# Nine softmax groups a pair, weight chunks converted partly by Prelu passes, and a new order of steps

## Chip, cores and metric

The kernel runs on one core of one Trainium2 chip. The metric is the device time of one execution in microseconds (us); a run's number is the median of several executions, and the number of this kernel is the median of three runs.

## What is computed

Two stages follow each other. Attention of 8 batches with 8 heads, 576 queries of 64 numbers each, where keys and values are first averaged over 8 neighbours, so that each query has 72 keys. Its output, 4608 rows of 512 numbers, then goes through a root-mean-square norm and a gated layer with 1536 hidden columns:

```python
k_p = k.reshape(B, H, 72, 8, D).mean(axis=3)           # B = H = 8, D = 64
v_p = v.reshape(B, H, 72, 8, D).mean(axis=3)
scores = scale * q @ k_p.T                             # 576 x 72 for each head
scores = scores - max(scores, axis=-1)
attn = exp(scores); attn = attn / (sum(attn, axis=-1) + 1e-9)
x = concat_heads(attn @ v_p)                           # 4608 x 512
xn = x / sqrt(mean(x * x, axis=-1) + 1e-6) * rms_g
g = xn @ w_gate                                        # 512 x 1536
val = xn @ w_val
out = (g * sigmoid(g) * val) @ w_out                   # 1536 x 512
```

The three weight matrices come as 64-bit floats, the rest as 32-bit floats.

## The kernel before

**Precision.** A product of 32-bit floats is made of three matmuls: each factor is split into a rounded high part ("hi", a copy into the type fp32r) and the remainder ("lo", a subtraction), and hi x hi, lo x hi and hi x lo are added in PSUM. The copy is mostly on ScalarE (ACT), the subtraction on GpSimd (POOL) or VectorE (DVE).

**Weights.** They arrive in 26 chunks, 16 of 512 and 10 of 1024 columns on 128 partitions (`CHUNKS`), as pairs of 32-bit words. A chunk takes six steps: `w_load` (a DMA, tile `wx`), `w_abs` (ACT, L316, the high word scaled by a power of two, into tile `wt`), `w_shift` (DVE, L320, three bits to the left), `w_low` (DVE, L324, the low word's bits joined in), `w_sign` (DVE, L328, the sign bit joined in), `w_hi` (ACT, L342, the rounded copy into `w`), and `w_lo` (L290, the subtraction, which POOL or DVE makes in `cut`; POOL does it in pieces of 256 columns, DVE whole).

**Attention.** A batch is four pairs of heads. Batches 0 and 1 (`EARLY`) use small matmuls to turn the probabilities (`s_pt`, then copies out of PSUM by `s_ptcopy`) and their own softmax steps (L426 to L466). For batches 2 to 7 a pair (b, p) goes through `sc` (`s_heads`, L476: ten matmuls of 72 columns, five groups of 128 rows for each head, the fifth of which repeats 64 rows), `mx`, `sb`, `ex`, `sm`, `nm` (max, subtraction, exponential on ACT, sum and reciprocal, product with the reciprocal; `nm` is `l_norm`, L506), `tr` (one 32 x 32 block transpose on DVE), `dm` (`l_place`, four DMAs to memory), `dp` (`l_collect`, one DMA back, tile `pt<-rows`), `av` (`s_av`, L558: half u of the tokens, two matmuls, one for each head on its own 64 columns of the array), `xc` (`l_xcopy`, ACT, L566) and `xd` (`l_xlast`, DVE).

**The gated layer.** Nine blocks of 512 tokens. Blocks 0 to 2 run as plain products, `mm1` (L1057, 512 columns a matmul; block 0's first part is `first_mm`, L1047) and `mm2` (L1091). Blocks 3 to 8 run in pairs with a scheme of seven products instead of eight (`product`, L893, and `product2`, L973), which needs sums of weight blocks: `w_whole`, `w_sum`, `w_sumlo` for one matrix and `v_whole`, `v_sum`, `v_sumlo` for the other (L755 to L806), each on POOL or DVE, stored to memory and read back through SyncE's queue (SP).

**What sets the order.** One written table, `ORDER`, for all engines: `run` reads it step by step, and every engine takes its instructions in that sequence, waiting by semaphores. A step that begins with `_` is from `first_steps`, the others from `later_steps`. In `either` a step has a usual engine and another one when its first letter is a capital: POOL is usual for `nm`, `jn`, `wt`, `wf`, `wl`, `zt`, `zf`, `zl`, and DVE for `sl`, `xl`, `lo`, `yl`, `fs`, `fl`. What stands behind `/` are buffers, behind `:` PSUM banks.

## Time and profile before

| | us |
|---|---|
| median of three runs | 975.05 (973.04 to 977.06) |
| the profiled execution, its own time | 969.89 |
| its span, first to last instruction | 968.1 |
| busy: TensorE matmul (PE) | 943.7, 97% |
| busy: DVE | 702.3, 73% |
| busy: POOL | 499.6, 52% |
| busy: ACT | 490.2, 51% |
| mean granted TensorE clock | 0.986 of full speed |

The profiled execution is one of several; its times are of that one, and 1.8 us of it lie outside its span. Busy shares are means over stages with different limits, so the tables below go by stretches of the span. The line of the engine's clock over 40 slices of 24.2 us begins with 7 and 7 tenths and is 9 from there on: the low clock stands in the first 50 us only.

### The profile page before, as it was taken

How to read it: one execution, taken by the hardware profiler on the slowest of the kernel's cores; microseconds unless marked ns; L12 is line 12 of the kernel's file. 1: busy time of each engine (PE TensorE's matmuls, PEld its weight loads, DVE VectorE, ACT ScalarE, POOL GpSimd, SP SyncE). 2: the span in 40 equal slices, each digit the busy share in tenths (PEclk: the TensorE clock that was granted, in tenths of full speed). 3: DMA queues.
4: the chain of work that ended last, by engine and by line, in shares of the span. 5: the costliest groups of instructions: out<-in, count | busy, mean ns of one | idle time of the engine just before them, and what ended most of it. 6: DMA issues, size and time to landing. Idle time of an engine off the chain costs nothing.

```text
span 968.1 us, 14177 instructions
## 1 busy us (share of the span) xinstructions
PE 943.7 (97%) x4670; PEld 748.7 (77%) x4670; DVE 702.3 (73%) x1134; ACT 490.2 (51%) x926; POOL 499.6 (52%) x618
## 2 busy tenths in 40 slices
...
GB/s 280 248 217 227 179 235 228 173 225 176 211 210 214 166 172 286 259 233 270 242 250 260 217 238 201 227 201 247 234 250 206 168 212 177 216 196 227 207 141 207
DMA packets 142296, 211.41 MB, mean 218 GB/s; under 512 B 12240, under 2 KB 78288, under 8 KB 140944
## 3 DMA queue, kind: packets, MB, share of 16 engines
...
## 4 chain that ended last, share of the span: by engine, by line
PE 72%; DVE 10%; DMA 7%; POOL 4%; ACT 3%; issue 3%; SPq 1%; ACTq 0%; DVEq 0%; POOLq 0%
PE pxy L893 33%; PE pf L973 15%; PE psg L1057 12%; PE po L1091 6%; PE psx L558 2%; PE pss L476 2%; DMA sum<-wt 2%; POOL fp L290 1%; DVE wt L324 1%; DMA wp<-blocks 1%; DVE wt L328 1%; DMA wp<-sum 1%; DVE wt L320 1%; DMA wx<-w 1%; POOL acc L290 1%
## 5 line engine op out<-in xcount | busy, mean ns | idle before, releaser
L893 PE MATMUL pxy<-xp,wp 128*128 128x512 f32 x1512 | 360.6, 390 | 1.5 <-DMA wp<-blocks 1.0
L893 PEld LDWEIGHTS pxy<-xp,wp 128*128 128x128 f32 x1512 | 282.4, 188 | 64.8 <-issue 3.6
L973 PE MATMUL pf<-fp,ring 128*128 128x512 f32 x756 | 189.7, 393 | 2.7 <-DMA ring<-vs 1.3
L1057 PE MATMUL psg<-xh,w 128*128 128x512 f32 x544 | 170.7, 394 | 2.2 <-ACT prob L439 1.0
L973 PEld LDWEIGHTS pf<-fp,ring 128*128 128x128 f32 x756 | 139.8, 188 | 38.9 <-issue 3.4
L1057 PEld LDWEIGHTS psg<-xh,w 128*128 128x128 f32 x544 | 100.4, 188 | 27.7 <-ACT prob L439 1.4
L1057 PE MATMUL psg<-xl,w 128*128 128x512 f32 x272 | 106.0, 390 | 0.0
L290 POOL TENSOR_TENSOR hl<-act,hh 128x256 fp32r<-128x256 f32 x58 | 46.2, 817 | 110.2 <-ACT hh L1073 90.8
L290 POOL TENSOR_TENSOR fp<-fs,fp 128x256 fp32r<-128x256 f32 x108 | 81.5, 781 | 41.1 <-ACT fp L946 37.3
L290 POOL TENSOR_TENSOR fp<-act,fp 128x256 fp32r<-128x256 f32 x72 | 55.1, 787 | 82.5 <-ACT fp L946 81.3
L290 POOL TENSOR_TENSOR w<-wt,w 128x256 fp32r<-128x256 f32 x50 | 54.8, 1123 | 36.1 <-ACT w L342 36.0
L1091 PE MATMUL po<-w,hh 128*128 128x512 f32 x288 | 72.9, 390 | 0.0
L1091 PEld LDWEIGHTS po<-w,hh 128*128 128x128 f32 x288 | 54.1, 188 | 11.7 <-DVE w L290 0.2
L290 POOL TENSOR_TENSOR fp<-hb,fp 128x256 fp32r<-128x256 f32 x68 | 55.2, 838 | 13.6 <-ACT fp L946 13.6
L1057 PEld LDWEIGHTS psg<-xl,w 128*128 128x128 f32 x272 | 51.1, 188 | 10.9 <-DVE xl L735 0.2
L1152 ACT COPY hb<-pxy 128x512 f32<-128x512 f32 x36 | 21.0, 586 | 72.8 <-PE pxy L893 72.8
L1159 DVE TENSOR_TENSOR u<-u,pxy 128x512 f32<-128x512 f32 x36 | 24.6, 685 | 39.3 <-PE pxy L893 39.1
L946 ACT CAST fp<-act 128x512 fp32r<-128x512 f32 x36 | 22.2, 619 | 58.3 <-DVE act L1160 49.1
L946 ACT CAST fp<-fs 128x512 fp32r<-128x512 f32 x54 | 33.1, 619 | 35.3 <-POOL fs L290 16.7
L290 POOL TENSOR_TENSOR fs<-act,hb 128x256 f32<-128x256 f32 x32 | 23.4, 751 | 50.4 <-DVE act L1160 27.7
L1153 DVE TENSOR_TENSOR u<-hb,pxy 128x512 f32<-128x512 f32 x36 | 24.6, 684 | 32.6 <-PE pxy L893 18.9
L1156 DVE TENSOR_TENSOR hb<-u,pxy 128x512 f32<-128x512 f32 x36 | 24.7, 687 | 28.7 <-PE pxy L893 27.8
...
## 6 DMA issues: line engine op xcount, KB each, us to landing
...
wp<-blocks SPq DMA_DIRECT2D x108, 256.0 KB
...
```

The costliest lines, as they stand in the source:

```text
L290: getattr(eng, op)(*(x[..., o:o + step] for x in (out, a, b)))
L476: nc.tensor.matmul(s["ps", h][:, t * SP:(t + 1) * SP], s["q"][r, o:o + P], s["pk"][r, :], start=True, stop=True)
L558: nc.tensor.matmul(ps[r, :n], s["pv"][:, r], x, start=True, stop=True)
L893: nc.tensor.matmul(ps[:, :NB], w[:, a, c, :], x[:, b, c, :], start=j == 0 and not more, stop=j == len(todo) - 1, skip_group_check=more)
L946: nc.scalar.copy(y[:, 0], f_source(i, k, j))
L973: nc.tensor.matmul(ps[c], w[:, a, c * P:(c + 1) * P], x[:, b], start=j == 0 and n == 0 and not more, stop=j == HALF - 1 and n == 2, skip_g ...
L1057: nc.tensor.matmul(ps[:, :NB], w[:, c, cols], x[c], start=(j == 0), stop=(j == len(todo) - 1))
L1091: nc.tensor.matmul(po[i][t], x[i, f][:, t * P:(t + 1) * P], w, start=(f == 0 and k == 0), stop=(f == NF - 1 and k == 2))
L1152: cp=lambda i, f: S_.copy(later(i, f), st["XY", i, f, 0]),
L1153: u2=lambda i, f: V.tensor_add(u2(i, f), later(i, f), st["XY", i, f, 1]),
L1156: c2=lambda i, f: V.tensor_sub(later(i, f), u3(i, f), st["XY", i, f, 4]),
L1159: v1=lambda i, f: V.tensor_add(u2(i, f), u2(i, f), st["XY", i, f, 5]),
```

## The change

Five things are changed at once.

1. For 21 of the 26 weight chunks (`BENT`; 8 of 1024 and 13 of 512 columns) the load starts three bytes into the row. `w_abs` becomes `w_start`, an ACT pass (Prelu with a bias from a tile) over the top byte, read as an 8-bit integer; `w_shift` becomes a second ACT pass that writes 32-bit integers and carries the sign along; `w_low` stays on DVE, and `w_sign` is nothing for these chunks.
2. The new step `_+` makes the rounded copy of a chunk on DVE instead of ACT (12 chunks), and `_=` makes the normalisation of an early pair on DVE instead of POOL.
3. The late pairs have nine groups of 128 rows instead of ten: four for each head, and one in which the last 64 rows of both heads share the partitions. `l_turn` turns nine groups, `l_place` is one DMA instead of four, `l_collect` three instead of one.
4. `s_av` takes for each half one matmul of 320 and one of 256 columns, where half 0 had two of 256 and half 1 two of 320; the copy of the last tokens (`l_xlast`) is one step per head instead of one per pair.
5. `ORDER` is another one up to the step `fh314`, and many steps in it have another engine. From there on it lists the same steps in the same sequence and on the same engines.

In counts: DVE has 1082 instructions where it had 1136, ACT 869 (868), POOL 664 (623), PE 4171 as before, and SP issues 749 DMAs (773).

```diff
-SEGS = ((0, 128), (128, 128), (256, 160), (416, 160))
+FULL = 4
+GROUPS = 2 * FULL + 1
...
+BENT = (0, 4, 5, 6, 7, 8, 10, 11, 12, 13, 14, 15, 16, 17, 19, 20, 21, 22, 23, 24, 25)
+SMALL = 2.0 ** -40
+UNIT = 2.0 ** 27
+SKIP = 3
...
-_zg:2 _q00 _k00 _q02 _K00 _S00:37 _k02 _K02 _S02:21 _M000 _l5/1 _a5/0 _M001 _b5 _c5 _v03 _E000 _k01 _q01 _K01 _k03 _q03
...
+_q00 _k00 _q02 _k02 _l5/0 _K00 _K02 _zg:3 _a5/0 _S00:21 _M001 _M000 _v03 _V03 _k01 _S02:47 _K01 _b5 _M020 _c5 _E000
...
+    shift = const.tile([P, 2], F32, name="shift")
+    nc.vector.memset(shift[:, 0:1], -56.0)
+    nc.vector.memset(shift[:, 1:2], 112.0 * SMALL * UNIT)
...
+        if n in BENT:
+            size = 8 * x.shape[1]
+            nc.sync.dma_start(x.rearrange("p n o -> p (n o)").bitcast(U8)[:, :size - SKIP], src.bitcast(U8)[:, SKIP:])
+            raw["x", n] = x[:, :, 0], x.bitcast(I8)[:, :, 4]
+        else:
+            nc.sync.dma_start(x.bitcast(I64).rearrange("p n o -> p (n o)"), src)
+            raw["x", n] = x[:, :, 0], x[:, :, 1]
+    def w_start(n):
         f, j = CHUNKS[n]
         if j == 3:
             t = space2(f + 1 if f < 3 else NF - 1 - f % 2, [P, 2 * WC], F32, f"wt{n}")
         else:
             t = two([P, WC], F32, tag="out", name=f"wt{n}")
         raw["t", n] = t
-        nc.scalar.activation(t, raw["x", n][1].bitcast(F32), AF.Abs, scale=W_SCALE)
+        if n in BENT:
+            nc.scalar.activation(t, raw["x", n][1], AF.Prelu, bias=shift[:, 0:1], alpha=SMALL)
+        else:
+            nc.scalar.activation(t, raw["x", n][1].bitcast(F32), AF.Abs, scale=W_SCALE)
     def w_shift(n):
-        u = raw["t", n].bitcast(U32)
-        nc.vector.tensor_scalar(u, u, 3, None, ALU.logical_shift_left)
+        t = raw["t", n]
+        if n in BENT:
+            nc.scalar.activation(t.bitcast(I32), t, AF.Prelu, scale=UNIT, bias=shift[:, 1:2], alpha=1.0 / SMALL)
+        else:
+            nc.vector.tensor_scalar(t.bitcast(U32), t.bitcast(U32), 3, None, ALU.logical_shift_left)
     def w_low(n):
         u = raw["t", n].bitcast(U32)
+        if n in BENT:
+            nc.vector.scalar_tensor_tensor(u, raw["x", n][0], 5, u, ALU.logical_shift_right, ALU.bitwise_or)
+            return
         nc.vector.scalar_tensor_tensor(u, raw["x", n][0], 29, u, ALU.logical_shift_right, ALU.bitwise_or)
     def w_sign(n):
+        if n in BENT:
+            return
         u = raw["t", n].bitcast(U32)
         nc.vector.scalar_tensor_tensor(u, raw["x", n][1], 0x80000000, u, ALU.bitwise_and, ALU.bitwise_or)
-    def w_hi(n):
+    def w_hi(n, copy=nc.scalar.copy):
...
+        copy(parts[:, 0, :], raw["t", n])
...
-        for t, o in enumerate(OFFS2):
+        for t, o in enumerate(OFFS2 if b in EARLY else OFFS2[:FULL]):
             for h in (0, 1):
                 r = slice(h * D, (h + 1) * D)
                 nc.tensor.matmul(s["ps", h][:, t * SP:(t + 1) * SP], s["q"][r, o:o + P], s["pk"][r, :],
                                  start=True, stop=True)
-
...
+    def l_groups(h, k=SP):
+        return prob[:, (FULL + 1) * h:FULL + 1 + FULL * h, :k]
     def l_scores(b, p, h):
-        n = len(OFFS2)
+        n = FULL + 1 - h
         return st[b, p]["ps", h][:, :n * SP].rearrange("p (t k) -> p t k", k=SP)
+    def l_two(b, p, h, tag):
+        return two([P, FULL + 1], F32, tag=f"{tag}{h}", name=f"{tag}{b}_{p}_{h}")[:, :FULL + 1 - h]
...
     def l_turn(b, p):
-        sq = st[b, p]["turned"] = two([P, 3, 2 * len(OFFS2), 32], F32, tag="st", name=f"sq{b}_{p}")
-        nc.vector.transpose(sq.rearrange("p b g j -> p g b j"), prob.rearrange("p g (b j) -> p g b j", b=3))
+        sq = st[b, p]["turned"] = two([P, 3, GROUPS, 32], F32, tag="st", name=f"sq{b}_{p}")
+        nc.vector.transpose(sq.rearrange("p b g j -> p g b j"),
+                            prob[:, :GROUPS].rearrange("p g (b j) -> p g b j", b=3))
     def l_place(b, p):
         sq = st[b, p]["turned"]
-        x = st[b, p]["rows"] = dram.tile([3, 32, 2 * S // 32, 32], F32, tag=f"rows{b}_{p}", name=f"rows{b}_{p}")
-        for a, (o, w) in enumerate(SEGS):
-            nc.sync.dma_start(x[:, :, o // 16:(o + w) // 16, :].rearrange("i r g j -> r i g j"),
-                              sq[32 * a:32 * (a + 1), :, :w // 16, :])
+        x = st[b, p]["rows"] = dram.tile([P, 3, GROUPS, 32], F32, tag=f"rows{b}_{p}", name=f"rows{b}_{p}")
+        nc.sync.dma_start(x, sq)
     def l_collect(b, p):
-        t = st[b, p]["pt"] = two([SP, 2 * S // 32, 32], F32, tag="ptf", name=f"pt{b}_{p}")
-        nc.sync.dma_start(t, st[b, p]["rows"].rearrange("i r g j -> (i r) g j")[:SP])
+        t = st[b, p]["pt"] = two([SP, 4, GROUPS, 32], F32, tag="ptf", name=f"pt{b}_{p}")
+        x = st[b, p]["rows"].rearrange("(a r) i g j -> i r a (g j)", a=4)
+        for i in range(3):
+            n = min(SP - 32 * i, 32)
+            nc.sync.dma_start(t[32 * i:32 * i + n].rearrange("r a g j -> r a (g j)"), x[i, :n])
...
+        t = s["pt"][:, 2 * u:2 * u + 2]
+        for h in (u, 1 - u):
             r = slice(h * D, (h + 1) * D)
-            if b in EARLY:
-                x = s["pt"][:, h, tok]
-            else:
-                x = s["pt"].rearrange("p (g h) j -> p h g j", h=2)[:, h, tok.start // 32:tok.stop // 32, :]
-            nc.tensor.matmul(ps[r, :n], s["pv"][:, r], x, start=True, stop=True)
+            first = h * (FULL + 1 - u)
+            n = FULL + (h == u)
+            o = u * (1 - h)
+            nc.tensor.matmul(l_wide(b, p, u)[r, :, o:o + n, :], s["pv"][:, r], t[:, :, first:first + n, :],
+                             start=True, stop=True)
+    def l_wide(b, p, u):
+        return st[b, p]["psx", u][:, :2 * (FULL + 1) * 32].rearrange("p (a t j) -> p a t j", a=2, j=32)
     def l_xcopy(b, p, u):
-        n = (256, S - 256)[u]
-        x = xraw[b][:, p, :]
-        y = x[:, :512].rearrange("p (t a j) -> p a t j", a=4, j=32)[:, 2 * u:2 * u + 2]
-        z = st[b, p]["psx", u][:, :n].rearrange("p (a t j) -> p a t j", a=2, j=32)
-        nc.scalar.mul(y, z[:, :, :4, :], 1.0 / POOL)
-    def l_xlast(b, p):
-        n = S - 256
-        z = st[b, p]["psx", 1][:, :n].rearrange("p (a t j) -> p a t j", a=2, j=32)
-        nc.vector.tensor_scalar(xraw[b][:, p, 512:].rearrange("p (a j) -> p a j", a=2), z[:, :, 4, :], 1.0 / POOL, None,
-                                ALU.mult)
+        y = xraw[b][:, p, :512].rearrange("p (t a j) -> p a t j", a=4, j=32)[:, 2 * u:2 * u + 2]
+        nc.scalar.mul(y, l_wide(b, p, u)[:, :, u:u + FULL, :], 1.0 / POOL)
+    def l_xlast(b, p, h):
+        r = slice(h * D, (h + 1) * D)
+        nc.vector.tensor_scalar(xraw[b][r, p, 512:].rearrange("p (a j) -> p a j", a=2),
+                                l_wide(b, p, h)[r, :, (1 - h) * FULL, :], 1.0 / POOL, None, ALU.mult)
...
+            **{"+": lambda n: w_hi(n, V.tensor_copy), "=": lambda b, p, h: s_norm(b, p, h, V)},
```

**The first weight chunk on DVE.** The rows are DVE's, in its own sequence, around the steps of chunk 5, the first to be loaded (`wx5` is the loaded tile, `wt5` the converted one; `pss`, `early` and `main` belong to the early softmax, `own` and `v0` to the pooling of keys and values). Before:

```order
L426 TENSOR_REDUCE early_87<-pss0_0_0_117 128x5
L426 TENSOR_REDUCE early_87<-pss0_0_1_118 128x5
L320 TENSOR_SCALAR wt5_147<-wt5_147 128x512
L324 SCALAR_TENSOR_TENSOR wt5_147<-wx5_145,wt5_147 128x512
L408 TENSOR_REDUCE own1_165<-main1_161 128x72
L328 SCALAR_TENSOR_TENSOR wt5_147<-wx5_145,wt5_147 128x512
L426 TENSOR_REDUCE early_87<-pss0_2_0_132 128x5
L446 TENSOR_TENSOR main0_108<-pss0_0_1_118,early_87 128x5x72
```

After:

```order
L459 TENSOR_REDUCE early_90<-pss0_0_1_128 128x5
L459 TENSOR_REDUCE early_90<-pss0_0_0_127 128x5
L450 TENSOR_REDUCE own3_143<-v0_3_141 72x128
L441 TENSOR_REDUCE own1_160<-main1_145 128x72
L459 TENSOR_REDUCE early_90<-pss0_2_0_148 128x5
L353 SCALAR_TENSOR_TENSOR wt5_125<-wx5_102,wt5_125 128x512
L479 TENSOR_TENSOR main0_94<-pss0_0_1_128,early_90 128x5x72
```

Of the three weight steps on DVE one is left, and it stands behind two pooling sums instead of ahead of one.

**The same chunk on ACT.** The rows are ACT's, from the chunk's first pass to its rounded copy (`CAST`; L437 to L441 of before and L470 to L474 of after are the early exponentials). Before:

```order
L316 ACTIVATE wt5_147<-wx5_145 128x512
L437 ACTIVATE early_87<-early_87 128x5
L439 ACTIVATE main0_108,early_87<-pss0_0_0_117,early_87 128x72 x5
L441 ACTIVATE early_87<-early_87,tiny_85 128x5
L342 CAST w2_1_173<-wt5_147 128x512
```

After:

```order
L339 ACTIVATE wt5_125<-wx5_102,shift_87 128x512
L346 ACTIVATE wt5_125<-wt5_125,shift_87 128x512
L470 ACTIVATE early_90<-early_90 128x5
L472 ACTIVATE main0_94,early_90<-pss0_0_0_127,early_90 128x72 x5
L474 ACTIVATE early_90<-early_90,tiny_85 128x5
L470 ACTIVATE early_90<-early_90 128x5
L472 ACTIVATE main2_98,early_90<-pss0_2_0_148,early_90 128x72 x5
L474 ACTIVATE early_90<-early_90,tiny_85 128x5
L484 ACTIVATE main0_94<-main0_94 128x5x72
L484 ACTIVATE main2_98<-main2_98 128x5x72
L375 CAST w2_1_237<-wt5_125 128x512
```

There are two passes over the chunk ahead of the softmax steps, and the copy stands behind the exponentials of two heads instead of one.

**Two late pairs on PE.** The rows are PE's at pairs 0 and 1 of batch 2, between a `po` step of block 1 and the next `psg` step (`psx` is the output of `av`, `pt` the turned probabilities, `pv` the pooled values). Before:

```order
L1091 MATMUL po1_3_1998<-w2_1_173,hh1_1_2014 128x512 x2
L558 MATMUL psx2_0_0_2048<-pt2_0_1799,pv2_0_1077 64x256 x2
L558 MATMUL psx2_0_1_2058<-pt2_0_1799,pv2_0_1077 64x320 x2
L558 MATMUL psx2_1_1_2064<-pt2_1_2011,pv2_1_1533 64x320 x2
L558 MATMUL psx2_1_0_2086<-pt2_1_2011,pv2_1_1533 64x256 x2
L1057 MATMUL psg1_3_0_2094<-xh1_0_1756,w1_3_617 128x512 x2
```

After:

```order
L1140 MATMUL po1_3_1921<-w2_1_237,hh1_1_1940 128x512 x2
L606 MATMUL psx2_0_0_2005<-pt2_0_1822,pv2_0_1093 64x320
L606 MATMUL psx2_0_0_2005<-pt2_0_1822,pv2_0_1093 64x2x128
L606 MATMUL psx2_0_1_2013<-pt2_0_1822,pv2_0_1093 64x320
L606 MATMUL psx2_0_1_2013<-pt2_0_1822,pv2_0_1093 64x2x128
L606 MATMUL psx2_1_1_2019<-pt2_1_1951,pv2_1_1487 64x320
L606 MATMUL psx2_1_1_2019<-pt2_1_1951,pv2_1_1487 64x2x128
L606 MATMUL psx2_1_0_2028<-pt2_1_1951,pv2_1_1487 64x320
L606 MATMUL psx2_1_0_2028<-pt2_1_1951,pv2_1_1487 64x2x128
L1106 MATMUL psg1_3_0_2034<-xh1_0_1754,w1_3_644 128x512 x2
```

Each half now has one matmul of each width.

## Rows read from the trace of the kernel before

**Rows 1.** Busy times by stretch.

```profile
core 0: us, PE busy (x) PEld busy (x) DVE busy (x) ACT busy (x) POOL busy (x), PEclk, DMA share, GB/s
0.00:20.00 20.00, 14.49 (x118) 13.34 (x118) 12.13 (x25) 10.24 (x44) 3.06 (x13) 0.84 0.91 292
20.00:40.00 20.00, 16.09 (x98) 10.53 (x98) 19.86 (x40) 19.34 (x67) 14.29 (x14) 0.67 0.65 215
40.00:104.00 64.00, 62.47 (x317) 48.24 (x316) 61.34 (x87) 47.97 (x113) 46.36 (x40) 0.94 0.69 222
104.00:440.00 336.00, 331.36 (x1727) 261.76 (x1726) 284.61 (x506) 194.63 (x349) 119.58 (x143) 1.00 0.70 214
440.00:600.00 160.00, 158.71 (x793) 124.21 (x792) 125.94 (x194) 87.63 (x142) 99.48 (x126) 1.00 0.79 240
600.00:968.00 368.00, 360.61 (x1625) 290.66 (x1624) 198.40 (x287) 130.39 (x215) 216.87 (x285) 1.00 0.66 208
```

**Rows 2.** The chain of waits, 0 to 70 us, its shares by line.

```profile
by line: DVE wt L324 12.7%; DVE wt L328 11.1%; DMA wx<-w 10.8%; DVE wt L320 9.8%; issue 9.5%; DVE early L426 5.0%; DVE own L417 4.5%; DVE xl L1021 4.3%; DVE w L290 3.5%; DVE early L455 2.8%; DVE main L446 2.6%; ACT prob L439 2.3%; DVE pk L4
```

**Rows 3.** DVE's groups by form, 0 to 104 us: count | busy us, mean ns | idle before.

```profile
L324 DVE SCALAR_TENSOR_TENSOR wt<-wx,wt 128x1024 uint32<-128x1024 uint32 x7 | 9.5, 1364 | 0.0
L328 DVE SCALAR_TENSOR_TENSOR wt<-wx,wt 128x1024 uint32<-128x1024 uint32 x7 | 8.6, 1232 | 0.0
L324 DVE SCALAR_TENSOR_TENSOR wt<-wx,wt 128x512 uint32<-128x512 uint32 x10 | 7.7, 774 | 0.1
L328 DVE SCALAR_TENSOR_TENSOR wt<-wx,wt 128x512 uint32<-128x512 uint32 x10 | 7.2, 728 | 0.0
L320 DVE TENSOR_SCALAR wt<-wt 128x1024 uint32<-128x1024 uint32 x7 | 6.6, 943 | 0.0
L320 DVE TENSOR_SCALAR wt<-wt 128x512 uint32<-128x512 uint32 x10 | 5.6, 566 | 1.8 <-ACT wt L316 1.6
L755 DVE TENSOR_TENSOR wsum<-w 128x1024 f32<-128x1024 f32 x3 | 4.1, 1356 | 0.0
L764 DVE TENSOR_TENSOR wsum<-wsum 128x256 f32<-128x256 f32 x6 | 3.9, 647 | 0.1
L290 DVE TENSOR_TENSOR w<-wt,w 128x512 fp32r<-128x512 f32 x2 | 2.4, 1224 | 0.0
```

**Rows 4.** Normalisations by form, whole span, on DVE and on POOL.

```profile
L506 DVE TENSOR_TENSOR prob<-prob,sm 128x360 f32<-128x360 f32 x46 | 26.2, 580 | 0.4
...
L466 POOL TENSOR_TENSOR prob<-prob,early 128x360 f32<-128x360 f32 x8 | 11.1, 1397 | 7.2 <-DVE early L461 5.8 <-ACT own L588 1.5
```

**Rows 5.** ACT's groups by form, whole span.

```profile
L342 ACT CAST w<-wt 128x1024 fp32r<-128x1024 f32 x10 | 10.5, 1048 | 2.6 <-DVE wt L328 2.5
L342 ACT CAST w<-wt 128x512 fp32r<-128x512 f32 x16 | 9.9, 618 | 1.5 <-DVE wt L328 1.3
...
L1102 ACT COPY o<-po 128x512 f32<-128x512 f32 x4 | 2.3, 587 | 4.7 <-DMA out<-o 2.9 <-DMA sum<-wt 1.8
...
L1098 ACT ACTIVATE o<-po,r 128x512 f32<-128x512 f32 x2 | 1.4, 685 | 0.8 <-DMA sum<-wt 0.8
```

**Rows 6.** PE's timeline at 40 us: start, duration, engine, line.

```profile
40.03 1.22 PE L1047 MATMUL psg<-xh,w 128*128 128x512 f32 x2
```

**Rows 7.** The chain over the whole span: start us, us, what.

```profile
225.34 2.97 PE po L1091 x12
...
236.47 2.72 PE po L1091 x12
...
347.44 2.94 PE psg L1057 x12
```

**Rows 8.** PE's groups by form, whole span, of the step `av`.

```profile
L558 PE MATMUL psx<-pt,pv 72*64 72x320 f32 x96 | 17.5, 450 | 1.5 <-DVE act L1069 0.9 <-DMA pt<-rows 0.6
L558 PE MATMUL psx<-pt,pv 72*64 72x256 f32 x96 | 15.3, 395 | 1.1 <-ACT xraw L566 0.9 <-DMA pt<-rows 0.2
```

**Rows 9.** The first weight load in the chain, and PE's wait for the collected tile.

```profile
3.08 7.55 DMA wx<-w
...
PE psx L558 <- DMA pt<-rows: 0.8, 3, 0.4
```

382 lines of the change are left out of this document (194 added, 188 removed).

## The prediction, made before the changed kernel ran

> **What bounds the kernel now.** I read the windows by stretch first, then the chain of waits, and after it the prices of single instructions. TensorE (PE) is busy 943.7 us by the sum of its six windows, of a span of 968.1 [rows 1], so no edit to another engine can return more than what PE loses. The same windows say where it loses. It stands idle 5.5 us in 0 to 20, 3.9 in 20 to 40, 1.5 in 40 to 104, 4.6 in 104 to 440, 1.3 in 440 to 600 and 7.4 behind that. On top of that comes the granted clock: 0.84, 0.67 and 0.94 of full speed in the first three stretches and 1.00 from there on. A stretch at 0.94 for 64 us does the work of 60.2, so 40 to 104 gives away another 3.8 us.
>
> Who makes PE lose? VectorE (DVE) is busy 19.9 of 20 us in 20 to 40 and 61.3 of 64 in 40 to 104. The chain followed back over the first 70 us runs almost wholly through DVE, and its three first entries there are the weight steps: 12.7 + 11.1 + 9.8 = 33.6% of 70 us, some 23.5 us [rows 2]. So up to 104 us DVE paces PE. From 104 to 440 DVE is at 284.6 of 336 us: not a bound by itself, but a step that PE wants is often still behind others in its queue. From 600 on DVE has 46% free, and nothing done to it pays. The two orders list the same steps in the same sequence from the step `fh314` on; by the number of 512-column matmuls ahead of it that is at about 509 us. So the change can move time in the first 509 us, and the rest is only shifted.
>
> **The change, part by part.** *Weight chunks.* I count to one place that both orders share: PE has 393 matmuls behind it, 197 of them 512 columns wide; in the trace of before that is where the third stretch ends, 104 us. Up to there DVE loses 6 shifts of 1024 and 7 of 512 columns, 6 x 0.943 + 7 x 0.566 = 9.6 us, and 6 and 7 of the two-input steps, at the mean of the low and the sign step 6 x 1.30 + 7 x 0.75 = 13.1 us [rows 3]: 22.7 off. It gains 9 rounding copies of weights that ACT made before. No row shows such a copy on DVE. The nearest is the shift, also one input and one output in SBUF: 5 x 0.943 + 4 x 0.566 = 7.0. If it went as the two-input step does it would be 5 x 1.36 + 4 x 0.77 = 9.9; I take 7.0. DVE also takes over 5 weight subtractions from POOL (5 x 1.22 = 6.1), 5 early normalisations (at the 0.58 of the late ones, 2.9 [rows 4]) and two PSUM copies (1.2, at the 0.59 of such a copy on ACT [rows 5]); 2 whole sums and 5 block sums leave it (2 x 1.36 + 5 x 0.65 = 5.9). Together DVE has 22.7 - 7.0 - 6.1 - 2.9 - 1.2 + 5.9 = 11.4 us less to do. Ahead of the first 512-column matmul (40.0 us [rows 6]) the same count gives 3 shifts and 4 two-input steps fewer (6.2), and 2 copies, 2 normalisations, 1 subtraction and 2 PSUM copies more (4.7), with 0.7 for a pooling step that comes later: about 2 us.
>
> What of this reaches PE? Its start can come 2 us earlier, since DVE leaves no gap in 20 to 40. From 40 to 104 PE can win back no more than its 1.5 idle and the 3.8 of clock, 5.4 rounded. I take half: the low clock of 0.67 in 20 to 40 stands where PE was idle 3.9 of 20 us, and the transposes and small matmuls, between which it was idle, stand there in both orders. **First term: -2.1 - 2.7 = -4.8**, between 0 and -7.5.
>
> ScalarE (ACT) pays for it. Up to the same place it has 13 second passes more, at the copy's duration plus what a pointer operand costs (0.685 - 0.587 = 0.10 [rows 5]): 6 x 1.15 + 7 x 0.72 = 11.9; 14 first passes with a bias, +1.4; 9 copies fewer, 5 x 1.05 + 4 x 0.62 = 7.7; about 1 off in small steps. Net +4.6 us on an engine that is busy 77.6 of 104 us, so it is covered, unless it falls into 20 to 40, where ACT has 0.7 us free. Ahead of the first large matmul ACT has 76 instructions where it had 80, which is why I book nothing. The table loads are 77 in both orders. The Trainium skill says to put multiplications, additions and relu on VectorE rather than ScalarE (ScalarE: Activation LUTs, Rules for kernel authors). By that rule alone the move is a loss of 11.9 against 9.6 us; the rows say that the engine that ends last here is DVE, so I follow them and keep the rule for a rival.
>
> *Nine groups instead of ten.* Each late pair has one head with four groups of 72 where it had five: 72 of 360 elements less in four DVE steps and one ACT step; 512 elements more cost the low step 1.364 - 0.774 = 0.59 us [rows 3], so that is some 0.08 us of the 0.58, 24 x 4 x 0.08 = 7.7 us of DVE over the kernel; the transpose is a tenth shorter, and the last-token copy becomes two. All of it lies behind 130 us. It belongs to the next term.
>
> *T sums, v sums and normalisations to POOL.* From 104 to 509 us DVE gives away a further 34 us by the same count, POOL takes some 40. POOL is busy 119.6 of 336 us in 104 to 440, so there is room. What would come late is a normalisation: 0.58 on DVE, 1.40 on POOL where DVE was full [rows 4]. The Trainium skill says that DVE and GpSimd hold a shared port pair for a whole instruction and the loser waits (SBUF — State Buffer, SBUF: two separate sides). The 1.40 agrees with it; by it POOL's new 40 us would also hold up DVE, which no row here separates.
>
> What PE can win in 104 to 440: the 4.6 idle, and short hitches that the windows don't count. In the chain a group of 12 matmuls takes 2.72 us undisturbed and 2.94 to 2.99 where it waited; between 222 and 350 us there are 10 such groups, the first and the last of which stand in [rows 7]. That is 10 x 0.23 in 128 us, 6.2 us over 336. Half of 10.8, since not every one hangs on DVE: **second term -5.4**, between 0 and -10.8.
>
> *AV matmuls.* Before, the two heads of a half had equal widths, 256 and 256 or 320 and 320, side by side. Now each half has one of 320 and one of 256, and ends with the longer. A half of 320 keeps PE 17.5 / 24 = 0.73 us, one of 256 15.3 / 24 = 0.64 [rows 8]. One half of each of 24 late pairs goes from the shorter to the longer: **third term +2.2**, between 0 and 2.2. The scores keep 10 matmuls of 72 columns a pair and cost nothing new.
>
> *DMA.* Placing takes 1 transfer where it took 4, collecting 3 where it took 1, 24 issues fewer in all. PE waited 0.8 us for the collected tile in the whole run [rows 9]: booked at 0, between -0.8 and +2, should the smaller rows make it late in a few pairs. The bent chunks are loaded from three bytes in; no row shows a load like that.
>
> **Sum:** -4.8 - 5.4 + 2.2 = -8.0 us. The profiled execution took 969.9 (span 968.1), 5.2 below the median of the three runs, 975.05; I set the sum against the median: **967.0 us**, and 961.9 for an execution like the profiled one.
>
> **Rivals.** *Only the start pays.* PE is at 62.5 of 64 and 331.4 of 336 us already; if its hitches come from its own switches between small and large matmuls, a lighter DVE doesn't help: -2.1 + 2.2 = 0, **975**. For it speaks that PE is nearly full, against it that DVE is too.
> *All of it pays.* -7.5 - 10.8 + 2.2 = -16, **959**. The order would have to be as good as the load allows.
> *ACT paces the front.* The second pass stands between the load and the DVE's low step, so a chunk goes through ACT twice and then waits for ACT again where the copy is not moved. If this ends last in 20 to 104 us, all 4.6 us fall on the path, the half clock lasts some 2 us longer, and the AV term stays: +8.8, **984**. It decides once over 0.7 us of added ACT work stands in 20 to 40, or once ACT's free 16 us of 40 to 104 lie behind waits. Against it: fewer ACT instructions ahead of the first large matmul.
> *The loads don't do what they are to.* If a chunk read from an odd byte takes twice its time, the first one, 7.55 us now [rows 9], shifts the start by up to 7.5 while the DMA engines are 91% busy: about **984** as well.
>
> **Chances.** The forecast 0.50 (its own range 961 to 973), only the start 0.22, all of it 0.10, ACT 0.10, loads 0.08. The range from 957 to 980 takes in the first three and the near half of the last two. A difference of 0.5% (4.9 us) is about what a measurement can tell from none: faster by more 0.57, within 0.25, slower 0.18.
>
> **What would show it.** Right: DVE clearly under 61 us in 40 to 104, the first 512-column matmul near 38 us, fewer 2.95-us groups between 222 and 350, AV halves all at 0.73 us. Wrong: ACT without a gap from 20 to 60 us with DVE waiting for its second pass; weight loads landing later than 10.6 us; PE idle in 104 to 440 unchanged, which would make the second term nothing; or PE waiting for the collected tile by several us.

## The result, and the profile after

The changed kernel takes **981.26 us** (median of 8 runs, 977.94 to 982.93); the kernel before, on the same chip, 974.99 (8 runs, 972.98 to 977.20). The ratio is **1.0060, 95% interval 1.0040 to 1.0079**. It is slower by 6.3 us, where 8 us faster was forecast, and 1.3 us above the range. The profiled execution took 981.75 (span 979.7), which is ordinary for this kernel; that of before, 969.89, was 5.2 below its median. So the two traces lie 11.9 us apart, and about half of that is the choice of execution. Wherever a few us matter, I use several traces of a kernel, or medians. A ratio is taken over all executions of both kernels, so it is not exactly the quotient of the two medians.

The windows of the changed kernel, with the columns of [rows 1]:

```profile
0.00:20.00 20.00, 15.42 (x128) 14.39 (x128) 12.36 (x31) 10.85 (x44) 1.75 (x12) 0.85 0.92 279
20.00:40.00 20.00, 15.62 (x94) 9.67 (x93) 19.27 (x39) 18.56 (x65) 10.06 (x12) 0.76 0.72 248
40.00:104.00 64.00, 63.38 (x323) 50.20 (x322) 53.41 (x77) 53.94 (x118) 35.12 (x36) 0.94 0.68 231
104.00:440.00 336.00, 330.01 (x1705) 258.52 (x1704) 251.14 (x436) 192.81 (x347) 155.52 (x193) 0.99 0.69 212
440.00:600.00 160.00, 155.53 (x771) 120.81 (x770) 124.06 (x199) 82.52 (x134) 91.40 (x113) 1.00 0.74 228
600.00:979.00 379.00, 369.70 (x1661) 297.25 (x1659) 204.83 (x302) 136.66 (x224) 224.94 (x294) 1.00 0.65 207
```

Against [rows 1], DVE is relieved as forecast: 53.4 us where it had 61.3 in 40 to 104, 251 where it had 285 in 104 to 440. PE did not follow. Its idle time fell from 1.5 to 0.6 us in 40 to 104, but rose from 4.6 to 6.0 in 104 to 440 and from 1.3 to 4.5 in 440 to 600, a stretch of which over half is written almost the same in both orders. Almost: behind the step `fh314` the two lists are not equal, as the section on the change and the prediction have it. The eight `xd` steps of batches 6 and 7 are sixteen in the changed order, at other places; all the rest is the same.

Windows by the clock slide apart once one kernel is ahead. Counting work is steadier: the start of the n-th matmul of 512 columns, read off PE's timeline (us). "Again" is a second trace of the same program; f3 and g2 are experiments below. Ahead of n = 1, 193, 400, 1460 and all later n of the table the same other matmuls lie in both orders. Ahead of the 900th the changed order has the `av` matmuls of one half fewer, some 0.6 us, and they follow before the 1460th; ahead of the 49th it also has one half fewer (and two `psb` more), and ahead of the 320th one half more.

| n | before | before, again | after | after, again | f3 | g2 |
|---|---|---|---|---|---|---|
| 1 | 40.0 | 40.2 | 37.9 | 38.8 | 38.1 | 38.7 |
| 49 | 63.5 | 63.3 | 62.9 | 65.3 | 64.7 | 66.9 |
| 193 | 103.1 | 103.2 | 101.0 | 103.3 | 103.1 | 105.2 |
| 320 | 139.4 | 139.3 | 137.8 | 140.6 | 140.0 | 143.0 |
| 400 | 162.1 | 162.1 | 163.6 | 166.3 | 165.8 | 164.6 |
| 900 | 301.0 | 300.9 | 301.9 | 303.2 | 302.2 | 302.5 |
| 1460 | 450.0 | 449.6 | 453.5 | 456.8 | 451.2 | 453.0 |
| 1692 | 508.4 | 507.9 | 514.8 | 518.3 | 512.4 | 514.1 |
| 2400 | 688.1 | 687.5 | 698.3 | 700.6 | 693.1 | 695.1 |
| 3560 | 963.0 | 962.0 | 974.5 | 974.0 | 970.9 | 968.7 |

Three things stand in it. Of the 1.2 to 2.3 us gained at the first matmul nothing is left at the 49th in the second trace, nor in f3 and g2; in the first trace 2.1 us are still there at the 193rd. Between the 320th and the 400th the changed kernel needs 25.8 and 25.7 us where before needs 22.7. And behind the 1460th it loses some 6 us more up to the 2400th, about half of that behind the 1692nd, where the two orders differ in the `xd` steps alone.

**The front.** Another engine is the full one now. The windows 30 to 42 us, before:

```profile
30.00:42.00 12.00, 10.10 (x60) 5.98 (x59) 12.00 (x20) 11.71 (x29) 8.31 (x8) 0.78 0.60 219
```

and after:

```profile
30.00:42.00 12.00, 11.69 (x70) 6.96 (x67) 11.50 (x23) 12.00 (x28) 3.21 (x4) 0.86 0.84 276
```

DVE was without a gap, now ACT is; it was nearly full before. Both passes of a weight chunk stand on ACT (its groups by form, whole span; columns as in [rows 5]):

```profile
L339 ACT ACTIVATE wt<-wx,shift 128x1024 f32<-128x1024 int8 x8 | 9.9, 1243 | 5.7 <-DVE w L307 4.1 <-DMA wx<-w 1.7
L339 ACT ACTIVATE wt<-wx,shift 128x512 f32<-128x512 int8 x13 | 9.9, 776 | 10.7 <-DMA wx<-w 8.0 <-DMA sum<-wt 1.6 <-POOL w L307 0.7
L346 ACT ACTIVATE wt<-wt,shift 128x512 int32<-128x512 f32 x13 | 9.5, 731 | 0.3
L346 ACT ACTIVATE wt<-wt,shift 128x1024 int32<-128x1024 f32 x8 | 9.2, 1156 | 0.0
```

and DVE waits for the second one (DVE's groups by form, 0 to 104 us):

```profile
L353 DVE SCALAR_TENSOR_TENSOR wt<-wx,wt 128x1024 uint32<-128x1024 uint32 x6 | 8.9, 1489 | 0.5 <-ACT wt L346 0.5
...
L353 DVE SCALAR_TENSOR_TENSOR wt<-wx,wt 128x512 uint32<-128x512 uint32 x7 | 5.4, 767 | 1.6 <-ACT wt L346 1.6
L375 DVE CAST w<-wt 128x1024 fp32r<-128x1024 f32 x5 | 4.2, 840 | 0.0
L375 DVE CAST w<-wt 128x512 fp32r<-128x512 f32 x4 | 1.7, 414 | 0.0
```

PE's waits, whole span (us in total, times, longest):

```profile
PE pst L577 <- POOL main L499: 3.6, 2, 3.2
PE pss L509 <- ACT main L472: 3.1, 1, 3.1
...
PE psr L699 <- POOL acc L307: 1.7, 1, 1.7
...
PE pf L1022 <- DVE hb L1206: 1.2, 1, 1.2
...
PE psg L1106 <- DVE xraw L620: 1.1, 1, 1.1
```

The first two stand ahead of 40 us: PE waits for a normalisation of the early softmax on POOL and for its exponentials on ACT. But PE waited there before too. Its idle time ahead of the first large matmul is 8.6 to 9.8 us in six traces of the changed front (after, f1, f2, f3, e2, g2) and 9.3 to 10.7 us in four of the old front (before, g1, h3, g4). The other lines are the next subjects.

The lead is lost between the 1st and the 49th large matmul, and PE hardly waits there. What differs is the granted clock (windows between the two; h3 and g4 run the front of before):

| | before | g1 | h3 | g4 | after | f1 | f2 | f3 | e2 | g2 |
|---|---|---|---|---|---|---|---|---|---|---|
| length, us | 23.5 | 23.1 | 27.1 | 27.5 | 25.0 | 26.5 | 25.0 | 26.6 | 28.1 | 28.2 |
| PE idle, us | 0.1 | 0.1 | 0.1 | 0.1 | 0.8 | 0.7 | 0.9 | 0.7 | 0.9 | 1.1 |
| granted clock | 0.83 | 0.85 | 0.72 | 0.70 | 0.80 | 0.74 | 0.80 | 0.74 | 0.70 | 0.70 |

The busy time times the clock is 19.0 to 19.6 us in all ten, so the length follows from the clock and at most 1 us of idle time. The windows 52 to 60 us, before:

```profile
52.00:56.00 4.00, 4.00 (x25) 3.40 (x25) 4.00 (x6) 2.69 (x6) 4.00 (x1) 1.00 0.53 127
56.00:60.00 4.00, 4.00 (x34) 2.61 (x32) 4.00 (x8) 3.71 (x6) 4.00 (x4) 1.00 0.91 342
```

and in g2:

```profile
52.00:56.00 4.00, 3.77 (x25) 3.57 (x24) 3.27 (x5) 2.63 (x6) 4.00 (x3) 0.50 0.22 70
56.00:60.00 4.00, 4.00 (x12) 3.12 (x12) 3.30 (x6) 3.87 (x4) 2.59 (x3) 0.54 0.45 154
```

Why the clock comes up early in one execution and late in another is not shown: the old front has 0.83 and 0.85 in two traces, 0.72 and 0.70 in two others.

**The sum of squares.** The third line is a wait at 145 us that before did not have. PE's ten `psr` matmuls (L699, the row sums of block 1's squares, step `_P10`) stand ahead of the step `_o8` now; before they stood behind all of that product. They need POOL's sums (timeline: start, duration, engine, line):

```profile
141.89 3.53 POOL L307 TENSOR_TENSOR acc<-acc,sq 128x288 f32<-128x288 f32 x2 [0.97 <-ACT sq L654]
...
145.47 0.83 PE L699 MATMUL psr<-one,acc 128*128 128x1 f32 x6 [1.71 <-POOL acc L307]
```

One of the two POOL sums took 2.765 us, where the median of the sixteen is 0.808. DVE was busy at the time, but it was just as busy beside the sum ahead of it, which took 0.81. PE is busy 0.53 of 2 us there, and behind it the clock stands at half (windows; POOL is full in both):

```profile
144.00:146.00 2.00, 0.53 (x5) 0.53 (x5) 1.70 (x3) 1.58 (x2) 2.00 (x2) 1.00 0.82 224
...
148.00:150.00 2.00, 2.00 (x6) 1.62 (x5) 2.00 (x4) 1.73 (x3) 2.00 (x3) 0.50 1.01 331
```

**The last-token copy.** It was one DVE instruction a pair; now it is one per half. Of the two copies that read one PSUM tile and write into one tile `xraw`, the one that stands later in `ORDER` waits for the earlier, on the other engine; over which of the two tiles, no run shows. Before, DVE's copy stood behind ACT's in 8 of 24 places, now it does in 33 of 48, in 18 of them right behind it. Its source view after:

```profile
L620 DVE TENSOR_SCALAR xraw<-psx x48: 199/219/229, 199.1 to 758.2; 64x64 f32<-64x64 f32 x48
...
its engine sat idle before it (us, times) until:
  ACT xraw L615: 21.7, 12
  PE psx L606: 1.4, 3
```

and before:

```profile
L571 DVE TENSOR_SCALAR xraw<-psx x24: 208/219/226, 199.7 to 747.7; 128x64 f32<-128x64 f32 x24
its engine sat idle before it (us, times) until:
  PE psx L558: 6.0, 7
  ACT xraw L566: 1.4, 2
who waited for it (us, times):
  ACT xraw L566: 11.1, 10
```

A copy of 0.22 us holds up DVE for 21.7 us in twelve places, and all that is queued behind it; before, ACT waited 11.1 us for DVE's copy. Behind 570 us, where only the `xd` steps differ, this reaches PE (timeline of the kernel after):

```profile
570.85 0.23 DVE L620 TENSOR_SCALAR xraw<-psx 64x64 f32<-64x64 f32 x1 [2.01 <-ACT xraw L615]
...
576.82 0.21 DVE L620 TENSOR_SCALAR xraw<-psx 64x64 f32<-64x64 f32 x1
...
577.06 0.69 ACT L654 ACTIVATE sq<-xraw 128x576 f32<-128x576 f32 x1 [3.23 <-DVE xraw L620]
...
577.78 1.02 DVE L307 TENSOR_TENSOR acc<-acc,sq 128x576 f32<-128x576 f32 x1 [0.75 <-ACT sq L654]
...
579.50 0.69 DVE L1206 TENSOR_TENSOR hb<-u,pxy 128x512 f32<-128x512 f32 x1
...
580.24 0.50 PE L1022 MATMUL pf<-fp,ring 128*128 128x512 f32 x1 [1.24 <-DVE hb L1206]
```

DVE waits 2.01 us for ACT's copy and has no gap from there to the `xd` at 576.8 us. That one comes late, ACT waits 3.23 us for it, DVE 0.75 for ACT's square, and the `hb` that PE wants (the 1.2 in PE's waits) comes late.

PE's waits from 510 to 700 us in the other traces bear this out. The one for `hb` (1.1 to 1.2 us), one of 0.5 for DVE's `u` and one of 0.4 for the copy itself stand in all four traces where the copy is on DVE behind ACT's (after, f1, e2, e1). None of the three stands in the five where it is on ACT (f3, g2, g3, g4, h1), nor in the kernel before (before, g1).

### The profile page after: what moved, and what is told of

Same layout as the page of the kernel before. It is cut to its first block, busy times and chain, and to the rows that moved or that the text cites. A ratio compares the mean times of both kernels' runs of the same rounds, so it can differ in the third digit from the quotient of the medians.

```text
span 979.7 us, 14153 instructions
## 1 busy us (share of the span) xinstructions
PE 949.6 (97%) x4670; PEld 750.8 (77%) x4670; DVE 665.1 (68%) x1080; ACT 495.3 (51%) x927; POOL 518.8 (53%) x659
## 4 chain that ended last, share of the span: by engine, by line
PE 57%; DVE 10%; DMA 9%; POOL 4%; ACT 2%; issue 2%; SPq 1%; DVEq 0%; ACTq 0%; POOLq 0%
PE pxy L942 28%; PE pf L1022 15%; PE psg L1106 7%; PE po L1140 3%; PE psx L606 2%; PE pss L509 2%; DMA pt<-rows 1%; POOL fp L307 1%; DMA v<-vN 1%; DMA sum<-wt 1%; DMA wp<-sum 1%; POOL xp L307 1%; DMA ring<-vs 1%; DVE sq L552 1%; DMA ring<-vB 1%
## 5 line engine op out<-in xcount | busy, mean ns | idle before, releaser
L995 ACT CAST fp<-act 128x512 fp32r<-128x512 f32 x36 | 22.2, 619 | 59.2 <-DVE act L1210 50.0
L307 POOL TENSOR_TENSOR hl<-act,hh 128x256 fp32r<-128x256 f32 x40 | 30.7, 787 | 31.5 <-ACT hh L1122 15.2
L822 POOL TENSOR_TENSOR wt<-wsum,wt 128x256 fp32r<-128x256 f32 x28 | 23.1, 830 | 43.3 <-ACT wt L818 41.3
L1207 ACT ACTIVATE hb<-hb 128x512 f32<-128x512 f32 x36 | 22.7, 632 | 45.1 <-DVE hb L1206 45.0
L1203 DVE TENSOR_TENSOR u<-hb,pxy 128x512 f32<-128x512 f32 x36 | 24.6, 684 | 30.1 <-PE pxy L942 19.6
L307 POOL TENSOR_TENSOR fs<-act,hb 128x256 f32<-128x256 f32 x28 | 20.3, 745 | 43.1 <-DVE act L1210 26.2
```

What stands on the lines that cost most here:

```text
L307: getattr(eng, op)(*(x[..., o:min(o + step, size)] for x in (out, a, b)))
L822: eng.tensor_sub(y[:, 1], place(f, f"T{k}"), y[:, 0].bitcast(F32))
L995: nc.scalar.copy(y[:, 0], f_source(i, k, j))
L1203: u2=lambda i, f: V.tensor_add(u2(i, f), later(i, f), st["XY", i, f, 1]),
L1207: sw=lambda i, f: S_.activation(later(i, f), later(i, f), AF.Silu),
```

## The experiments

Every ratio is against the kernel before, measured beside it on the same chip, whose median lay between 971.4 and 971.9 us. The groups e, f, g and h were measured apart from each other, on three chips. All of them compute the whole result.

**First four: code, order, passes, engines.** e1 has the changed kernel's code under the order and the engines of before; `xd` is split, and each half stands behind its `xc`.

```diff
-... ORDER and engine letters of the changed kernel ...
+... ORDER and engine letters of the kernel before ...
-... xc211 ... xc210 ... xd21 ...
+... xc211 xd211 xc210 xd210 ...
```

> All code of the changed kernel (two Prelu passes for 21 chunks, nine groups, one 320 and one 256 in each half, loads from three bytes in), but the sequence and the engines of the kernel before; the last-token step stands right behind the copy of its half. Theory A, the order and the engine choices make the loss and the code is a gain: DVE has some 23 us less up to 104 us, the front gains 2 to 5 us, nothing new waits: 970 to 974. Rival B, the passes on ACT, the odd loads or the AV shapes make the loss: 979 or more, and ACT then ends last in 20 to 104 us.

Measured: 982.24 us, ratio 1.0112 [1.0085, 1.0138]. The new code alone, in the old order, is no faster than the whole change. But e1 has a place for `xd` that neither kernel has, right behind its `xc` in all 48 cases, and g3 below, with that copy on ACT, has lost most of e1's excess. So e1 by itself does not clear the new order.

e2 moves one step of the changed kernel, the ten `psr` matmuls, behind `_o8`.

```diff
-_Wk sb200 _P10:0 _u9 _o8 _lo/0
+_Wk sb200 _u9 _o8 _P10:0 _lo/0
```

> The changed kernel with one step moved: the ten small matmuls that add up the squares of batch 1 stand behind the 12 matmuls of the following output step instead of ahead of them. In the trace of the changed kernel PE sits idle there for 2.5 us until POOL has ended a sum, and the clock is at half behind it for some 4 us. Theory A, this place costs 2.5 idle and 2 of clock, less 1 that the kernel before lost there too: 981.3 - 3.5 = 977.8. Rival: PE waits for the next late step instead and nothing is won: 981.

Measured: 979.51 us, 1.0074 [1.0045, 1.0104]; the 320th to the 400th matmul take 21.6 us in its trace, where the changed kernel has 25.8. From the 193rd to the 400th, with the same work in both orders, before takes 59.0 us, the changed kernel 62.6, e2 61.3 and g2 below 59.4. The wait is real and cured. In the median it is 1.5 us against f1 (below, the changed kernel again, on another chip), and the intervals of the two overlap.

e3 takes the Prelu passes out and keeps the new order; the missing sign steps are put behind the low steps.

```diff
-BENT = (0, 4, 5, 6, 7, 8, 10, 11, 12, 13, 14, 15, 16, 17, 19, 20, 21, 22, 23, 24, 25)
+BENT = ()
-... _b5 _M020 _c5 _E000 ...
+... _b5 _M020 _c5 _d5 _E000 ...
```

> The changed kernel's order with no chunk bent: loads from the row's start, Abs on ACT, shift, low and sign steps on DVE for all 26 chunks. Theory A, the Prelu passes are a gain, and DVE needs the 23 us up to 104: 985 to 992, with the first 512-column matmul at 40 us or later. Rival B, the passes and the loads are what costs: 977 or less.

Measured: 1000.86 us, 1.0311 [1.0290, 1.0331]. Its window from 40 to 104 us is full on DVE, and PE loses there:

```profile
40.00:104.00 64.00, 58.01 (x272) 45.28 (x273) 61.52 (x88) 35.51 (x77) 26.80 (x24) 0.84 0.56 190
```

e4 keeps the new sequence and gives 137 of its later steps back to the engines that had them before.

```diff
-... _m103 wt0/1 _u0 ... _w6 wf00 _d9 ... wl03 ...
+... _m103 Wt0/1 _u0 ... _w6 Wf00 _d9 ... Wl03 ...
```

> The changed kernel's sequence with the engines of the kernel before for 137 steps of the later part (the sums of weights and the normalisations that went from DVE to POOL, and the few that went the other way). Theory C, steps on POOL come late and hold DVE up, so DVE's gain of 34 us is lost between 104 and 509 us: 976 to 978, with the losses behind 440 us gone. Rival: the sequence was laid out for these engines and DVE is late again: 985 or more.

Measured: 1003.11 us, 1.0333 [1.0306, 1.0359]. PE loses it from 104 to 440 us, 318.5 busy of 336 where the changed kernel has 330:

```profile
104.00:440.00 336.00, 318.54 (x1589) 245.28 (x1588) 250.84 (x465) 178.75 (x329) 103.33 (x126) 0.96 0.61 194
```

e3 and e4 together: the new order needs the passes and the engines, each for some 20 us. I read this as an order that is laid out for a lighter DVE and spends the relief; another order for either was not tried.

**The last-token copy.** f1 is the changed kernel once more, for a second trace and a ratio beside f2 and f3.

> The changed kernel itself, as a measure beside the three others on the same chip and for a second trace. Over the kernel before by 0.4 to 0.8%. In the second trace PE should lose again where the order is that of before: at the 1728th 512-column matmul some 0.6 us and at the 1926th some 1.3 us, both waits for DVE, if these are the change's doing; if they come and go with an execution's transfers, they are gone.

Measured: 980.99 us, 1.0094 [1.0061, 1.0127]; the 1.2 us for `hb` stand in its trace again. f2 moves each `xd` that stood behind the `xc` of its half ahead of it (33, where the expectation says 36); f4 does the same with all 48 in e1.

```diff
-... av201:3 hi12/0 xc201 ... xd201 ...
+... av201:3 hi12/0 xd201 xc201 ...
```

> The changed kernel with each last-token copy on DVE ahead of the copy of the same half on ACT, where it stood behind it (36 of 48). In the trace of the changed kernel DVE sat idle 21.7 us in 12 waits for that ACT copy; before it was 1.4 us. Theory A: this wait makes DVE late for PE between 440 and 600 us, and it goes: the losses at the 1728th and 1926th matmul (0.6 and 1.3 us) and some 2 us between 450 and 510 us are gone, 3 to 5 us less than the changed kernel on this chip. Rival: DVE's idle time there is slack, PE's losses are late transfers: within 1 us of the changed kernel.

> All code of the changed kernel in the order and on the engines of the kernel before, as in an earlier run, but with each last-token copy ahead of the copy of its half. Theory A: the earlier run's losses behind 450 us go (4 to 5 us between the 1460th and the 1692nd matmul, 2 us behind), what stays is the front, which was 3.5 us longer there at the lower clock: 974 to 978 where the kernel before has 971.4. Rival: no gain over the earlier run, 982.

Measured: f2 987.58 us, 1.0158 [1.0131, 1.0186], 6.6 us worse than f1; f4 983.13, 1.0112 [1.0090, 1.0133], as e1. It was no cure, since the wait only changes sides. The copy's source view in f2:

```profile
its engine sat idle before it (us, times) until:
  PE psx L609: 24.5, 18
who waited for it (us, times):
  ACT xraw L618: 45.7, 31
```

DVE now waits for PE, and ACT waits for DVE. f3 takes the second engine away: the copy is made by ACT, and in `ORDER` each `xd` stands right behind the `xc` of its half (those moves are left out here).

```diff
-        nc.vector.tensor_scalar(xraw[b][r, p, 512:].rearrange("p (a j) -> p a j", a=2),
-                                l_wide(b, p, h)[r, :, (1 - h) * FULL, :], 1.0 / POOL, None, ALU.mult)
+        nc.scalar.mul(xraw[b][r, p, 512:].rearrange("p (a j) -> p a j", a=2),
+                      l_wide(b, p, h)[r, :, (1 - h) * FULL, :], 1.0 / POOL)
```

> The changed kernel with the last-token copy on ACT, right behind the copy of the same half, so that DVE neither makes it nor waits for it. Theory A: 3 to 5 us less than the changed kernel, as with the other cure, or 1 us better still, since DVE also loses 48 x 0.22 us of work. Rival (slack): no difference, or 1 us more, since ACT gets 48 x 0.2 us of work.

Measured: 977.10 us, 1.0054 [1.0031, 1.0077], 3.9 us better than f1, where the two intervals still overlap. ACT sits idle ahead of none of the 48 copies now (timeline of f3, two of them):

```profile
568.09 0.22 ACT L623 ACTIVATE xraw<-psx 64x64 f32<-64x64 f32 x1
...
569.31 0.22 ACT L623 ACTIVATE xraw<-psx 64x64 f32<-64x64 f32 x1
```

f3 also takes 48 x 0.22 us of work off DVE. What share that has in the 3.9 us no run separates; h3 below moves the copy in the kernel before, which gains nothing by it.

**Both cures, and the old order with them.** g1 is the kernel before once more. g2 is e2 and f3 in one. g3 is e1 with f3's copy, and g4 is g3 without the passes.

```diff
 g4 against g3
-BENT = (0, 4, 5, 6, 7, 8, 10, 11, 12, 13, 14, 15, 16, 17, 19, 20, 21, 22, 23, 24, 25)
+BENT = ()
```

> The kernel before itself, for a second trace of it. Ratio 1.000 within 0.004. Theory A, the change's losses are real: behind the 1692nd 512-column matmul PE again loses nothing at the 1728th and 1926th. Rival, the first trace was a lucky one and such losses come and go: 0.6 and 1.3 us stand there.

> The changed kernel with the two cures together: last-token copies on ACT (3.9 us faster than the changed kernel alone), and the sums of batch 1's squares behind the next output step (4.2 us less at that place in a trace). Theory A, the two places are independent: 981.0 - 3.9 - 3 = 974, still not under the kernel before (971.8 on that chip). Rival, the second cure only moves the wait: 977.

> All code of the changed kernel in the order and on the engines of the kernel before, with the last-token copy on ACT, so that the two waits found are out of it. Theory A, passes on ACT, nine groups and AV shapes are worth no more than 2 us even without those waits, since PE's front is paced by its clock and not by DVE's load: within 3 us of the kernel before (ratio 0.998 to 1.003). Rival: DVE's 23 us less up to 104 us pay as forecast: ratio 0.993 to 0.996. Other rival: the passes on ACT end last in the front: 1.005 or more, with the chain on ACT up to 60 us.

> As the run with all code in the old order and the last-token copy on ACT, but no chunk bent, so only nine groups, the new transfers and the new AV shapes are left of the change. Theory A: within 2 us of the kernel before (0.998 to 1.002), since its 8 us of DVE lie where DVE is no bound and AV costs at most 2 us. Against the run with the passes it gives what the passes alone do in the old order: faster than that one, if the passes on ACT cost the front; slower, if DVE's shorter work pays.

Measured: g1 970.44 us, 0.9984 [0.9963, 1.0005]; g2 974.99, 1.0028 [1.0003, 1.0054]; g3 975.67, 1.0038 [1.0018, 1.0058]; g4 976.09, 1.0025 [1.0000, 1.0050]. g2 is 2.1 us better than f3 (intervals overlapping), and a window shows where. 139 to 165 us, after:

```profile
139.00:165.00 26.00, 23.82 (x109) 19.18 (x109) 18.30 (x29) 15.52 (x25) 17.99 (x20) 0.93 0.73 221
```

and g2:

```profile
139.00:165.00 26.00, 26.00 (x143) 20.77 (x141) 19.29 (x31) 18.62 (x31) 20.67 (x23) 1.00 0.71 214
```

PE has no gap left and the full clock. In the old order the copy on ACT is worth about 7 us (e1 to g3), clear of noise, and the passes nothing that can be measured (g3, g4). With both cures the change is still behind the kernel before, by 3.1 us in the medians; the interval goes from 0.03% to 0.54%. In g1's trace PE again has none of the waits for DVE behind 510 us.

**Is it the clock in the front?** g2's clock is 0.53 from 12 to 30 us and that of before 0.55. h1 fills two gaps of g2 with idle matmuls (`_z`), h2 four of the kernel before; h3 makes the last-token copy of the kernel before on ACT, right behind its `xc`; h4 is h2 and h3.

```diff
 h1 against g2
-_K10/1 _l1 _S01:26 ... _E101 _T030:0
+_K10/1 _l1 _z7:5 _S01:26 ... _E101 _z4:0 _T030:0
 h2 against the kernel before
-_h5 _U001 _S01:64 ... _M021 _S03:20 ... _v00 _T001:0 ... _h2 _A010:6
+_h5 _U001 _z6:5 _S01:64 ... _M021 _z2:5 _S03:20 ... _v00 _z3:5 _T001:0 ... _h2 _z3:6 _A010:6
```

> The changed kernel with both cures, and idle 128-column matmuls in two of PE's gaps: 7 ahead of the early scores at 10.4 us (gap 3.1 to 3.3 us), 4 ahead of the transposes at 21 us (gap 3.2). Theory A, the clock takes the front's gain: the half clock from 12 to 30 us gets shorter and the times up to 104 us fall by 2 to 5 us, 970 to 973 where the kernel with both cures alone has 975.0. Rival B, waits on ACT's exponentials set the front whatever the clock: within 1 us of 975. Rival C, the added matmuls hold up the scores behind them: 976 to 978.

> The kernel before with idle 128-column matmuls in four of PE's gaps (6 at 10.5 us, 2 at 15.3, 3 at 22.3, 3 at 37.1). Theory A (clock): the half clock gets shorter, 2 to 5 us less than the kernel before, ratio 0.995 to 0.998, and that is faster than both kernels. Rival B: within 0.1%. Rival C: 1 to 3 us slower, since the gaps are not where they were once something else moves.

> The kernel before with its one last-token copy a pair on ACT, right behind the copy of the second half, where ACT waited 11.1 us in 10 waits for DVE's. Theory A, only the change made that copy cost PE something: within 1 us of the kernel before. Rival, the copy was late there too: 1 to 3 us faster, and then part of what the cure gave the changed kernel was no loss of the change.

> The two edits of the kernel before together (idle matmuls in four gaps, last-token copy on ACT), as a try at a version that beats both kernels. If both pay, 3 to 7 us less than the kernel before; if neither does, within 1 us.

Measured: h1 977.46 us, 1.0073 [1.0050, 1.0095]; h2 974.62, 1.0027 [1.0003, 1.0052]; h3 973.35, 1.0023 [0.9996, 1.0050]; h4 974.21, 1.0028 [1.0006, 1.0050]. The filling did what it should to the clock. 12 to 30 us in g2:

```profile
12.00:30.00 18.00, 12.34 (x83) 9.75 (x84) 17.50 (x39) 15.71 (x80) 6.94 (x9) 0.53 0.90 283
```

and in h1:

```profile
12.00:30.00 18.00, 11.66 (x97) 9.60 (x95) 17.51 (x39) 15.86 (x81) 6.80 (x8) 0.72 0.90 273
```

The clock rose to 0.72 (in h2 likewise, from 0.55), and neither kernel became faster; h1 is 2.5 us slower than g2 in the medians. DVE is busy 17.5 to 17.9 of 18 us there in all four traces, at either clock. The front did get shorter in h1: the clock from the 1st to the 49th large matmul is 0.86 where g2 has 0.70, and the 193rd starts at 102.4 us, 2.8 earlier than in g2 (in h2 at 103.9, before at 103.1). But the lead is not kept: h1 loses 2.2 us of it from the 400th to the 900th, and the 3560th starts at 968.7 us in both traces. So even a front won is not yet a kernel won here; what takes the lead away is open. h3 says that the copy on ACT is no improvement of its own in the kernel before: what it cures in the changed one is a wait that the change made.

## Why the prediction was wrong

**The first term: the start came, the -2.7 for 40 to 104 did not.** The durations were right: the second pass 0.731 and 1.156 us (0.72 and 1.15 expected), DVE's load in 40 to 104 well under 61. The copies on DVE were even cheaper, 0.414 and 0.840, than the 0.566 and 0.943 I took from the shift. The start came too: the first large matmul at 37.9 to 38.8 us in six traces, 39.7 to 40.2 in four of the old front, 1.5 us earlier on average (-2.1 forecast). What failed is the step "I take half" of the 1.5 us idle and the 3.8 us of clock. From the 1st to the 193rd large matmul six traces with the changed front take 63.1 to 66.5 us (mean 64.8), four with the old front 63.0 to 65.1 (mean 64.0). Some idle time came back behind the 49th (0.1 to 0.2 us left of 1.4 and 2.1 in before and g1; h3 and g4, which come there later, have none either), but ahead of it the clock, 0.70 to 0.80, was no better than that of the old front, 0.70 to 0.85, and gave away more than in the trace that the sum was made from. At the 193rd the six stand at 103.2 us, the four at 104.0: **the first term is about -1, inside a spread of 2 to 4 us, not -4.8**. A clock read from one execution was taken for a property of the order.

"I book nothing" for ACT was not the step that failed, as far as PE shows it. Up to 104 us ACT got 5.8 us more to do (4.6 forecast), it is without a gap from 30 to 42, and DVE waits for its second pass. But in 20 to 40 its load fell from 19.34 to 18.56 us, and PE's idle time ahead of the first large matmul did not grow. In the old order the passes cost nothing at the 193rd either: 105.1 us with them (g3), 105.0 without (g4). So the rival "ACT paces the front" had a fuller ACT right, but no price of it is shown; "only the start pays" had the price of the front nearly right. That the clock from 12 to 30 us holds the kernel, h1 and h2 speak against.

**The second term: -5.4 forecast, none found.** Its step was to read half of PE's idle time and hitches as hanging on DVE. From the 400th to the 1460th large matmul, with the same work in both orders, before takes 287.9 and 287.5 us; the traces of after, after again, f3 and g2 take 289.9, 290.5, 285.4 and 288.4. Up to the 900th alone they look 1.5 us faster than before, but 0.6 of that is the half of `av` that lies behind it now, and f2, e2 and h1, left out of that average, take 137.6, 138.6 and 140.1 where before takes 138.9. PE's idle time in 104 to 440 rose from 4.6 to 6.0, the sign that was to make the term nothing. The hitches are not fewer either: of the pairs of 512-column matmuls that follow each other directly, 9 start over 0.3 us apart between 222 and 350 us in before and in g1, 13 in after, f1, f3 and g2 (0.23 undisturbed). The prediction's own count of slow groups was nine, not ten, which makes its bound 10.3 and its half 5.2. The new order spends the relief of 34 us on DVE: with the old engines in it some 22 us are lost (e4 against f1), most of them from 104 to 440. The passes are alike: in the old order removing them changes nothing (g3, g4), in the new one it costs 20 us (e3). I read this as an order written for one load of the engines, which gives nothing back for a lighter one by itself; that is argued, not shown.

**"The change can move time in the first 509 us": not so.** It rested on equal lists from `fh314` on, and the `xd` steps differ there. From the 1692nd to the 2400th large matmul before takes 179.7 and 179.6 us, the changed kernel 183.5 and 182.3, with the copies on ACT 180.7 and 181.0 (f3, g2).

**Two waits that the prediction did not book.** "The last-token copy becomes two" went into a sum of DVE's work as if its 0.22 us were its price. Its price was its place: on two engines, one copy behind the other, 21.7 us of DVE standing still, 3.9 us on the end (f1 to f3; 7 in the old order, e1 to g3). The `psr` step's move was in the order, and I did not cost it: 1.5 to 2.1 us (e2 against f1, g2 against f3).

**The AV term.** A pair of matmuls of 320 and 256 columns takes 0.75 us by the timeline, whichever half, so the 0.73 forecast was about right for one half. But a half of two 256s stands only 0.1 us below it when it is alone (0.58 against 0.68 us to the next matmul), and two halves back to back take 1.12 to 1.19 us in both kernels. So it is at most about 1 us, not 2.2. g4 and h3 have the old order and the copy on ACT, and differ by the nine groups, the transfers, the shapes of `av` and the copy in two halves: 1.0025 and 1.0023, so together these cost nothing that can be measured.

**The rest was right.** The odd-byte loads cost nothing that shows: ACT takes up the first chunk at 10.2 us, before 10.6. PE waits 0.5 us for the collected tile in the whole run, 0.8 before; other traces have 0.3 to 2.0 of the change and 2.0 of the kernel before (g1), inside the bounds forecast.

**The account.** In f1 the change costs 9.2 us (980.99 against 971.79). The copy is 3.9 of it (f3), the sum of squares another 2.1 (g2), and 3.1 stay. Each step alone is hardly clear of noise; the two together are, 1.0094 [1.0061, 1.0127] against 1.0028 [1.0003, 1.0054]. What the 3.1 are is **open**. The AV pairs are up to 1. The copy on ACT may itself be part of it, as h3 has 1.0023 [0.9996, 1.0050] without any of the rest. And one loss stands in every trace of the changed order: from the 1460th to the 1692nd large matmul 60.0 to 63.3 us in seven traces (after, f1, f2, f3, e2, g2, h1), 58.3 or 58.4 in before, g1, h2 and h3, and 59.2 in h4. A wait of 1.0 us for POOL's `fp` near its end is in six of the seven (not f2), and there is none at that place in before; waits for the collected tile (1.4 in g2) are in it too. No run took one of them away. That the change costs 6.3 us in the first comparison and 9.2 in the second is no contradiction: the two intervals overlap.
